# Half-filled score matmuls as pairs of 64-row tiles, in a one-core attention block on Trainium2

## The chip, the core and the metric

The kernel runs on one core of one Trainium2 chip. TensorE (PE) multiplies and writes its results to PSUM, eight banks of 512 f32 per partition. VectorE (DVE) and ScalarE (ACT) read PSUM and work on SBUF. POOL and SP mostly issue DMAs here. The metric is device time in microseconds, the median of the timed runs of a kernel. Whatever differs by less than 0.3% counts as no change that this measurement can tell.

## The reference

Eight batches of 112 query rows attend over a cache of 512 keys, with 32 heads of width 192. The projections before and after the attention belong to it.

```
B, Sq, D = 8, 112, 640;  H, Sk, Dh = 32, 512, 192          # all bf16
q      = (x @ wq).reshape(B, Sq, H, Dh).transpose(0, 2, 1, 3)
scores = einsum("bhqd,bhkd->bhqk", q, k_cache) * Dh ** -0.5
p      = softmax(scores, axis=-1)
o      = einsum("bhqk,bhkd->bhqd", p, v_cache)
out    = o.transpose(0, 2, 1, 3).reshape(B, Sq, H * Dh) @ wo
```

## The kernel before

The 32 heads are split into four groups of eight. Within a head group the kernel goes over the eight batches, and within a batch over four pairs of heads: 4 x 8 x 4 = 128 pairs, numbered `ip`. K and V come in groups of two pairs (four heads), 64 groups in all, each into one of six `kt` and six `vt` buffers.

All five engines run programs that are written out by hand in a fixed order. `DEFAULT_ORDERS` gives for each engine a list of stages with a lag, and in period i an engine runs each stage for pair i + lag. TensorE's list is S(i), PT0(i-1), PV(i-2), PT1(i-1), O(i-3), Q(i+2). VectorE's is smax0(i), smax1(i), qc(i+1), evacpT1(i-1), recip(i), diag0(i), diag1(i), oacc(i-3). ScalarE's is evacQ(i+1), evacpT0(i-1), exp0(i), exp1(i), evacPV(i-2). Semaphores hold the engines together: an instruction waits until a count of another engine's steps is reached, and whatever stands behind it on its engine waits with it. Nothing is reordered by a scheduler.

The stages of one pair (two heads h = 0, 1):

- **Q** (L262): 15 matmuls with 112 columns make the queries of both heads, 384 rows in three chunks, in PSUM bank 5. ScalarE copies them to slots 0 to 2 of the buffer `qs` (evacQ, L272).
- **qc** (L323 to L326): a head's 192 rows don't fill whole chunks of 128. The middle chunk, slot 1, holds the last 64 rows of head 0 in partitions 0 to 63 and the first 64 rows of head 1 in partitions 64 to 127. VectorE therefore moves half-chunks across partitions into slots 3 to 6 (L324, L325), and copies the halves of slot 1 into slots 7 and 8 (L323, L326). The other halves of slots 7, 8, 3 and 6 that a score matmul reads as padding are zeros: `qs` is set to zero at the start, and nothing is ever written there.
- **S** (L166 to L169): the scores. The transposing DMA leaves K in `kt[:, parity, m, :]` with keys of even and odd parity in the two halves of one 384-row stack: m = 0 holds 128 rows of the even keys, m = 2 holds 128 rows of the odd keys, and m = 1 holds the remaining 64 rows of the even keys in partitions 0 to 63 and of the odd keys in partitions 64 to 127. For each head there are four matmuls with 256 columns: even keys with m = 0 and m = 1 (L166, L167), odd keys with m = 2 and m = 1 (L168, L169). The two with m = 1 run over 128 partitions, but half of their stationary operand is zeros. Head h has bank h to itself.
- **smax0, smax1** (L332): VectorE reads bank h, scales it into `s_sb` and takes the row minimum. **exp** (ACT, L284) makes `p_sb` and the row sums. **recip** (L344) and **diag** (L308) make a diagonal matrix of the inverse sums.
- **PT** (L182): four matmuls per head transpose and scale the probabilities. ScalarE (L278) and VectorE (L338, evacpT1) copy them out.
- **PV** (L200, L206): eight matmuls with full 128-column tiles, then eight whose output has 64 partitions. The latter go in pairs to two column tiles of the array (h = 0 to partitions 0 to 63, h = 1 to 64 to 127). The profile writes their shape as 128\*64. ScalarE copies the result out (L291).
- **O** (L234, L235): six matmuls with `wo`, summed over four pairs; every fourth pair VectorE adds the sum to an accumulator (oacc, L375; L377 in the last head group).

S waits for the copies of its queries (`dQC`), for its K (`mK`) and for VectorE's reads of the banks of the pair before (`dSM`: the first head needs smax0 of the pair before, the second smax1). SP issues the K transposes (L477) and V loads (L489) alternately; a buffer's next load waits until its last use has passed. POOL issues the weights.

Of the kernel before, what the change touches and what calls it, by code (L numbers as in the profile page):

```python
# [9 lines left out]
ALU = mybir.AluOpType  # L10
# [10 lines left out]
def build_mha_kernel(nc, x, k_cache, v_cache, wq, wo, out, cfg=None):  # L21
    cfg = dict(cfg or {})
    B, SQ, D = x.shape
# [11 lines left out]
    G = 4  # L35
    NGRP = NPAIR // 2
    scale = float(DH) ** -0.5
# [14 lines left out]
    NSS = cfg.get("NSS", 4)  # L52
# [10 lines left out]

    EA = [0, 5]
    OC = [4, 2]
    ET = [7, 6]
    OH = [3, 8]
    NSLOT = 9

    with ExitStack() as es:  # L70
        def sb(name, shape, dt):
            return es.enter_context(nc.sbuf_tensor(name, shape, dt))

        def sem(name):
            return es.enter_context(nc.semaphore(name))
# [12 lines left out]
        kt = [sb(f"kt{j}", [128, 2, 3, G * 128], BF16) for j in range(NKB)]  # L88
        vt = [sb(f"vt{j}", [128, G, 768], BF16) for j in range(NVB)]
        qs = sb("qs", [128, NQ, NSLOT, SQ], BF16)  # L90
        s_sb = sb("s_sb", [SQ, NSS, SK], F32)
# [9 lines left out]
        ps = es.enter_context(nc.psum_tensor("ps", [128, 8, 512], F32))  # L101

        sS = sem("sS"); sPT = sem("sPT"); sPV = sem("sPV"); sO = sem("sO"); sQ = sem("sQ")
        dSM = sem("dSM"); dDG = sem("dDG"); dQC = sem("dQC"); dPTE = sem("dPTE"); dOA = sem("dOA"); dRC = sem("dRC")
# [41 lines left out]
        def W(eng, s, v):  # L146
            if v > 0:
                eng.wait_ge(s, v)
# [4 lines left out]
        def pe_S(pe, i):  # L153
            g = i // 2
            kb = g % NKB
            qb = i % NQ
            W(pe, dQC, i + 1)
            W(pe, mK[kb], 16 * (g // NKB + 1))
            for h in range(2):
                Hh = 2 * i + h  # L160
                u = Hh % G
                W(pe, dSM, Hh - 1)
                bk = ps[0:SQ, h, :]
                ktb = kt[kb]
                cs = slice(u * 128, (u + 1) * 128)
                pe.matmul(bk[:, 0:256], qs[:, qb, EA[h], :], ktb[:, :, 0, cs], start=True, stop=False)  # L166
                pe.matmul(bk[:, 0:256], qs[:, qb, ET[h], :], ktb[:, :, 1, cs], start=False, stop=True)  # L167
                pe.matmul(bk[:, 256:512], qs[:, qb, OC[h], :], ktb[:, :, 2, cs], start=True, stop=False)  # L168
                pe.matmul(bk[:, 256:512], qs[:, qb, OH[h], :], ktb[:, :, 1, cs], start=False, stop=True).then_inc(sS, 1)  # L169

        def pe_PT(pe, ip, h):
            Hh = 2 * ip + h
# [74 lines left out]
        def pe_Q(pe, ip):  # L247
# [11 lines left out]
            for c in range(3):  # L259
                for dc in range(DC):  # L260
# [3 lines left out]
            mm.then_inc(sQ, 1)  # L264

        PE_STAGES = dict(S=pe_S, PT0=lambda pe, ip: pe_PT(pe, ip, 0), PT1=lambda pe, ip: pe_PT(pe, ip, 1),
                         PV=pe_PV, O=pe_O, Q=pe_Q, OF=pe_OF)

# [44 lines left out]
        def dve_qc(eng, ip, as_i32=False):  # L313
            on_pool = as_i32
            if on_pool != (ip >= QC_SWITCH):
                return
            qb = ip % NQ
            if on_pool and ip == QC_SWITCH:
                W(eng, dQC, ip)
            W(eng, aQE, ip + 1)  # L320
            v = (lambda ap: ap.bitcast(mybir.dt.int32)) if as_i32 else (lambda ap: ap)
            f2 = lambda ap: v(ap.rearrange("p a b -> p (a b)"))
            eng.tensor_copy(v(qs[0:64, qb, 7, :]), v(qs[0:64, qb, 1, :]))  # L323
            eng.tensor_copy(f2(qs[0:64, qb, 4:7, :]), f2(qs[64:128, qb, 0:3, :]))  # L324
            eng.tensor_copy(f2(qs[64:128, qb, 3:6, :]), f2(qs[0:64, qb, 0:3, :]))  # L325
            eng.tensor_copy(v(qs[64:128, qb, 8, :]), v(qs[64:128, qb, 1, :])).then_inc(dQC, 1)  # L326

        def dve_smax(dve, i, h):
            Hh = 2 * i + h
            W(dve, sS, Hh + 1)  # L330
            W(dve, aEX, Hh - NSS + 1)
            dve.tensor_scalar(s_sb[:, Hh % NSS, :], ps[0:SQ, h, :], -scale, None, op0=ALU.mult,  # L332
                              op1=ALU.min, accum_out=nmx[:, Hh % NS:Hh % NS + 1]).then_inc(dSM, 1)

        def dve_evacpT1(dve, ip):
# [10 lines left out]
        def dve_oacc(dve, ip):  # L346
# [22 lines left out]
            for k, (src, cs) in enumerate(parts):  # L369
# [6 lines left out]
                else:  # L376
                    ins = dve.tensor_tensor(o_out[:, b, cs], src, acc[:, b, cs], op=ALU.add)  # L377
            ins.then_inc(dOA, 1)

        DVE_STAGES = dict(diag0=lambda d, ip: dve_diag(d, ip, 0), diag1=lambda d, ip: dve_diag(d, ip, 1),  # L380
                          qc=dve_qc, smax0=lambda d, i: dve_smax(d, i, 0), smax1=lambda d, i: dve_smax(d, i, 1),
                          evacpT1=dve_evacpT1, recip=dve_recip, oacc=dve_oacc)

# [153 lines left out]
        def _(gp):  # L537
# [107 lines left out]
            def pool_o(gp_, i):  # L645
                for fn in odmas.get(i, []):
                    fn()

            POOL_STAGES = dict(qc=lambda e, ip: dve_qc(e, ip, as_i32=True))
            pend = max(dmas) + 1  # L650
            wl = max([lag for st, lag in orders["POOL"] if st == "w"] + [0])
# [12 lines left out]
def bass_standalone__mha_block_cached__near_ridge_kernel(  # L664
    nc: bass.Bass,
    x: bass.AP,
    k_cache: bass.AP,
    v_cache: bass.AP,
    wq: bass.AP,
    wo: bass.AP,  # L670
    out: bass.AP,
):
    return build_mha_kernel(nc, x, k_cache, v_cache, wq, wo, out)
# [28 lines left out]
```

## Time and profile before

| what | value |
|---|---|
| timed runs | 500.34, 501.38, 502.07 us; median 501.38 |
| profiled execution: span from first to last instruction | 499.2 us, mean granted TensorE clock 0.999 |
| median of the timed runs less that span | 2.1 us |
| spacing of S(i) to S(i+1) on TensorE, median | 3.65 us |
| score matmuls L166, L167, L168, L169 | 256 each, recorded 275, 273, 272, 273 ns (medians) |
| qc copies L323, L324, L325, L326 in one period | 178, 243, 242, 189 ns |
| smax L332 | 685 ns, and an 82 ns read of the accumulator that overlaps the next instruction |

The profiler lists no total of the profiled execution apart from its span; the 2.1 us are what this document takes as lying around the span.

How to read it. In the timeline each row has its start in us from the span's start, its length in us, the engine, the line, the operation, what it writes and reads, the shape, and how many instructions the row merges; a note in square brackets tells of idle time ahead of it and of what ended that. TensorE's matmuls are pipelined, so a matmul recorded with 273 ns can start 109 ns after the one before; what a matmul costs is the distance between starts. Loads of the stationary operand are listed as an engine of their own (PEld).

### The profile page before, as it was taken

What the parts mean: (1) busy time and instruction counts of PE and PEld (TensorE: products, weight loads), DVE (VectorE), ACT (ScalarE), POOL (GpSimd) and SP (SyncE); (2) the same over time, 40 slices, a digit from 0 to 9 for tenths busy, and PEclk for the clock granted to TensorE, in tenths of its full rate; (3) what the DMA queues carried; (4) which work ended last, traced back from release to release, by engine and by line L of the source; (5) the groups of instructions that cost most, each with busy time, mean ns of one, the idle gap of its engine ahead of it and who ended that gap; (6) DMA issues with size and microseconds to landing.
All of it is one profiled execution on the core that took longest, in us unless ns stands there. A gap on an engine that the chain in (4) does not pass through costs nothing.

```text
span 499.2 us, 18678 instructions
## 1 busy us (share of the span) xinstructions
PE 479.0 (96%) x6824; PEld 418.9 (84%) x6824; DVE 446.6 (89%) x1610; ACT 355.1 (71%) x898; POOL 71.5 (14%) x133
## 2 busy tenths in 40 slices
PE   1799999999999999999999999999999999999995
PEld 1788888888888888888888888888888888888884
DVE  2589999998999999999999999999999999999994
ACT  1277777777777777777777777777777777777773
POOL 7110133131000133131000122322000000000000
PEclk9999999999999999999999999999999999999999
DMA  9999999999999999999999999999999999999000
GB/s 227 305 285 239 244 256 274 249 265 292 237 249 263 281 261 259 245 265 251 239 247 236 259 290 279 240 282 260 233 272 254 255 260 255 238 258 261 3 14 25
DMA packets 239738, 119.90 MB, mean 240 GB/s; under 512 B 201840, under 2 KB 236480, under 8 KB 239648
## 3 DMA queue, kind: packets, MB, share of 16 engines
q1 hardware_dynamic: 233472, 101.82, 94.4%
q0 software_dynamic: 6176, 16.88, 11.3%
q8 instruction: 56, 0.92, 0.8%
q14 instruction: 34, 0.28, 0.2%
HBM read 67.21 MB, written 1.15 MB: 137 GB/s over the span
## 4 chain that ended last, share of the span: by engine, by line
PE 93%; DMA 2%; issue 1%; DVE 1%; POOL 1%; ACT 0%; DVEq 0%; POOLq 0%; ACTq 0%
PE ps L262 19%; PE ps L234 16%; PE ps L182 13%; PE ps L200 10%; PE ps L206 8%; PE ps L166 6%; PE ps L169 6%; PE ps L167 6%; PE ps L168 6%; PE ps L235 4%; DMA wq_sb<-in_wq_dram 2%; DVE xT_sb L409 1%; POOL wq_sb L578 0%; DVE s_sb L332 0%; DVE o_out L377 0%
## 5 line engine op out<-in xcount | busy, mean ns | idle before, releaser
L284 ACT ACTIVATE p_sb<-s_sb,nmx 112x512 bf16<-112x512 f32 x256 | 181.6, 712 | 3.1 <-DVE s_sb L332 2.1
L332 DVE TENSOR_SCALAR_CACHE_REDUCE s_sb<-ps 112x512 f32<-112x512 f32 x256 | 166.3, 686 | 16.2 <-PE ps L169 14.0
L278 ACT ACTIVATE pT_sb<-ps 128x448 bf16<-128x448 f32 x128 | 69.5, 543 | 88.4 <-PE ps L182 88.4
L262 PE MATMUL ps<-xT_sb,wq_sb 128*128 128x112 bf16 x1920 | 118.0, 215 | 5.2 <-DMA wq_sb<-in_wq_dram 5.2
L234 PE MATMUL ps<-wo_sb,oT_sb 128*112 128x512 bf16 x384 | 118.3, 380 | 0.0
L262 PEld LDWEIGHTS ps<-xT_sb,wq_sb 128*128 128x128 bf16 x1920 | 103.8, 99 | 16.7 <-DMA wq_sb<-in_wq_dram 4.4
L182 PE MATMUL ps<-dg,p_sb 112*128 112x112 bf16 x1024 | 94.0, 214 | 1.8 <-ACT p_sb L284 1.6
L272 ACT ACTIVATE qs<-ps 128x336 bf16<-128x336 f32 x128 | 57.6, 450 | 45.0 <-PE ps L262 41.8
L338 DVE CAST pT_sb<-ps 128x448 bf16<-128x448 f32 x128 | 79.9, 624 | 5.3 <-PE ps L182 1.4
L235 PE MATMUL ps<-wo_sb,oT_sb 128*112 128x128 bf16 x384 | 83.9, 219 | 0.0
L182 PEld LDWEIGHTS ps<-dg,p_sb 112*128 112x128 bf16 x1024 | 64.5, 98 | 14.4 <-ACT p_sb L284 1.9
L166 PE MATMUL ps<-kt,qs 128*112 128x256 bf16 x256 | 70.8, 277 | 2.5 <-issue 1.9
L200 PE MATMUL ps<-pT_sb,vt 128*128 128x112 bf16 x1024 | 71.8, 213 | 0.1
L167 PE MATMUL ps<-kt,qs 128*112 128x256 bf16 x256 | 70.4, 275 | 0.0
L169 PE MATMUL ps<-kt,qs 128*112 128x256 bf16 x256 | 70.4, 275 | 0.0
L168 PE MATMUL ps<-kt,qs 128*112 128x256 bf16 x256 | 70.3, 275 | 0.0
L234 PEld LDWEIGHTS ps<-wo_sb,oT_sb 128*112 128x112 bf16 x384 | 49.7, 129 | 22.3
L581 POOL DMA_DIRECT2D wq_sb<-in_wq_dram x60 | 32.1, 539 | 188.5 <-DMA kt<-in_k_cache_dram 182.4
L308 DVE TENSOR_SCALAR dg<-ident,rinv 112x112 bf16<-112x112 bf16 x256 | 52.9, 249 | 5.0 <-issue 0.5
L200 PEld LDWEIGHTS ps<-pT_sb,vt 128*128 128x128 bf16 x1024 | 56.5, 98 | 0.9 <-issue 0.5
L291 ACT ACTIVATE oT_sb<-ps 128x336 bf16<-128x336 f32 x128 | 55.3, 432 | 1.7 <-PE ps L206 1.7
L235 PEld LDWEIGHTS ps<-wo_sb,oT_sb 128*112 128x112 bf16 x384 | 50.0, 130 | 0.0
(38 smaller groups left out, 498.5 us busy)
## 6 DMA issues: line engine op xcount, KB each, us to landing
vt<-in_v_cache_dram SPq DMA_DIRECT2D x64, 768.0 KB, 5.8
wq_sb<-in_wq_dram POOLq DMA_DIRECT2D x60, 96.0 KB, 5.3
wo_sb<-in_wo_dram POOLq DMA_DIRECT2D x24, 160.0 KB, 5.6
wo_sb<-in_wo_dram POOLq DMA_DIRECT2D x32, 80.0 KB, 5.1
wq_sb<-in_wq_dram POOLq DMA_DIRECT2D x4, 480.0 KB, 10.2
wo_sb<-in_wo_dram POOLq DMA_DIRECT2D x4, 320.0 KB, 10.9
out_dram<-o_out SPq DMA_DIRECT2D x8, 140.0 KB, 4.4
kt<-in_k_cache_dram SPq DMA_TRANSPOSE x64, 9.9
```

Of the source, the lines that this page charges most:

```text
L166: pe.matmul(bk[:, 0:256], qs[:, qb, EA[h], :], ktb[:, :, 0, cs], start=True, stop=False)
L167: pe.matmul(bk[:, 0:256], qs[:, qb, ET[h], :], ktb[:, :, 1, cs], start=False, stop=True)
L168: pe.matmul(bk[:, 256:512], qs[:, qb, OC[h], :], ktb[:, :, 2, cs], start=True, stop=False)
L169: pe.matmul(bk[:, 256:512], qs[:, qb, OH[h], :], ktb[:, :, 1, cs], start=False, stop=True).then_inc(sS, 1)
L182: mm = pe.matmul(ps[:, 2 + h, j * SQ:(j + 1) * SQ], p_sb[:, pslot, j * 128:(j + 1) * 128], dg[:, dslot, :], start=True, stop=True)
L200: pe.matmul(ps[:, 4, oc * SQ:(oc + 1) * SQ], vtb[:, u, q * 192: q * 192 + 128], pT_sb[:, ptb, h, j * SQ:(j + 1) * SQ], start=(j == 0), sto ...
L234: pe.matmul(ps[0:SQ, 6, :], oT_sb[:, ob, c, :], wo_sb[:, wb, 3 * lp + c, 0:512], start=first, stop=last)
L235: mm = pe.matmul(ps[0:SQ, 7, 0:128], oT_sb[:, ob, c, :], wo_sb[:, wb, 3 * lp + c, 512:640], start=first, stop=last)
L262: mm = pe.matmul(ps[:, 5, c * SQ:(c + 1) * SQ], lhsT, xT_sb[:, dc, b * SQ:(b + 1) * SQ], start=(dc == 0), stop=(dc == DC - 1))
L284: act.activation(p_sb[:, Hh % NP, :], s_sb[:, Hh % NSS, :], ACTF.Exp, bias=nmx[:, Hh % NS:Hh % NS + 1], scale=-1.0, accum_out=rsum[:, Hh % ...
L332: dve.tensor_scalar(s_sb[:, Hh % NSS, :], ps[0:SQ, h, :], -scale, None, op0=ALU.mult, op1=ALU.min, accum_out=nmx[:, Hh % NS:Hh % NS + 1]). ...
L338: dve.tensor_copy(pT_sb[:, ip % NPT, 1, :], ps[:, 3, 0:4 * SQ]).then_inc(dPTE, 1)
```

## The change

The two halves of chunk m = 1 are no longer padded to 128 rows. The four matmuls with m = 1 become 64-row matmuls: for the even keys on partitions 0 to 63, for the odd keys on partitions 64 to 127. The even keys of both heads go to bank 0, the odd keys of both to bank 1 (head h in columns 256h to 256h + 255), so that the two 64-row tiles of a pair write to different banks. The order within S becomes: four full matmuls (even and odd keys of head 0, then of head 1), then the four 64-row ones (even, odd, even, odd). Only the first matmul of a bank carries the start flag.

Both banks are complete only after the last matmul of S. So smax0 and smax1 both wait for all of S, each reads 256 columns of both banks, and S waits ahead of its first matmul for both smax of the pair before. The copies to slots 7 and 8 go, and `qs` has seven slots.

```diff
-    ET = [7, 6]
-    OH = [3, 8]
-    NSLOT = 9
+    ET = [1, 6]
+    OH = [3, 1]
+    NSLOT = 7
...
+            ktb = kt[kb]
+            cs = [slice(u * 128, (u + 1) * 128) for u in ((2 * i) % G, (2 * i + 1) % G)]
+            W(pe, dSM, 2 * i)
             for h in range(2):
-                Hh = 2 * i + h
-                u = Hh % G
-                W(pe, dSM, Hh - 1)
-                bk = ps[0:SQ, h, :]
-                ktb = kt[kb]
-                cs = slice(u * 128, (u + 1) * 128)
-                pe.matmul(bk[:, 0:256], qs[:, qb, EA[h], :], ktb[:, :, 0, cs], start=True, stop=False)
-                pe.matmul(bk[:, 0:256], qs[:, qb, ET[h], :], ktb[:, :, 1, cs], start=False, stop=True)
-                pe.matmul(bk[:, 256:512], qs[:, qb, OC[h], :], ktb[:, :, 2, cs], start=True, stop=False)
-                pe.matmul(bk[:, 256:512], qs[:, qb, OH[h], :], ktb[:, :, 1, cs], start=False, stop=True).then_inc(sS, 1)
+                hs = slice(h * 256, (h + 1) * 256)
+                pe.matmul(ps[0:SQ, 0, hs], qs[:, qb, EA[h], :], ktb[:, :, 0, cs[h]], start=(h == 0), stop=False,
+                          skip_group_check=True)
+                pe.matmul(ps[0:SQ, 1, hs], qs[:, qb, OC[h], :], ktb[:, :, 2, cs[h]], start=(h == 0), stop=False,
+                          skip_group_check=True)
+            for h in range(2):
+                hs = slice(h * 256, (h + 1) * 256)
+                m1 = pe.matmul(ps[0:SQ, 0, hs], qs[0:64, qb, ET[h], :], ktb[0:64, :, 1, cs[h]],
+                               start=False, stop=True, skip_group_check=True)
+                m2 = pe.matmul(ps[0:SQ, 1, hs], qs[64:128, qb, OH[h], :], ktb[64:128, :, 1, cs[h]],
+                               start=False, stop=True, skip_group_check=True)
+            m1.then_inc(sS, 1)
+            m2.then_inc(sS, 1)
...
-            eng.tensor_copy(v(qs[0:64, qb, 7, :]), v(qs[0:64, qb, 1, :]))
             eng.tensor_copy(f2(qs[0:64, qb, 4:7, :]), f2(qs[64:128, qb, 0:3, :]))
-            eng.tensor_copy(f2(qs[64:128, qb, 3:6, :]), f2(qs[0:64, qb, 0:3, :]))
-            eng.tensor_copy(v(qs[64:128, qb, 8, :]), v(qs[64:128, qb, 1, :])).then_inc(dQC, 1)
+            eng.tensor_copy(f2(qs[64:128, qb, 3:6, :]), f2(qs[0:64, qb, 0:3, :])).then_inc(dQC, 1)
...
-            W(dve, sS, Hh + 1)
+            W(dve, sS, 2 * i + 2)
...
-            dve.tensor_scalar(s_sb[:, Hh % NSS, :], ps[0:SQ, h, :], -scale, None, op0=ALU.mult,
+            dve.tensor_scalar(s_sb[:, Hh % NSS, :].rearrange("p (e c) -> p e c", e=2), ps[0:SQ, 0:2, h * 256:(h + 1) * 256], -scale, None, op0=ALU.mult,
```

## The prediction

> **What bounds the kernel now.** I read the page's busy shares first, then the chain that ended last, then one period of TensorE and of VectorE in the timeline, then the landings of K.
>
> ```profile
> PE 479.0 (96%) x6824; PEld 418.9 (84%) x6824; DVE 446.6 (89%) x1610; ACT 355.1 (71%) x898; POOL 71.5 (14%) x133
> ...
> PE 93%; DMA 2%; issue 1%; DVE 1%; POOL 1%; ACT 0%; DVEq 0%; POOLq 0%; ACTq 0%
> ```
>
> TensorE carries 93% of the chain. VectorE's 89% comes close, so it has to be asked whether it becomes the bound. The timeline of TensorE, one period:
>
> ```profile
> 241.87 0.28 PE L166 MATMUL ps<-kt,qs 128*112 128x256 bf16 x1
> 241.98 0.27 PE L167 MATMUL ps<-kt,qs 128*112 128x256 bf16 x1
> ...
> 242.75 0.36 PE L182 MATMUL ps<-dg,p_sb 112*128 112x112 bf16 x4
> 242.94 0.56 PE L200 MATMUL ps<-pT_sb,vt 128*128 128x112 bf16 x8
> 243.44 0.39 PE L206 MATMUL ps<-pT_sb,vt 128*64 128x112 bf16 x8
> 243.75 0.37 PE L182 MATMUL ps<-dg,p_sb 112*128 112x112 bf16 x4
> 243.96 0.38 PE L234 MATMUL ps<-wo_sb,oT_sb 128*112 128x512 bf16 x1
> ...
> 245.52 0.28 PE L166 MATMUL ps<-kt,qs 128*112 128x256 bf16 x1
> ```
>
> The reader is to see the distances between starts. The eight score matmuls take 242.75 - 241.87 = 0.88 us, 0.11 each (from single starts: 0.109), with no gap. A 112-column matmul costs 0.049 (the four of L182 from 242.75 to 242.94). The period is 3.65 us.
>
> The same rows hold the one place where this kernel already changes its tiles: L206 runs in pairs on two column tiles. Eight L200 at 0.049 would end at 243.33; L206 starts at 243.44, so going in costs **0.10**. L206 then needs 0.31 for four pairs; four starts at 0.049 are 0.20, and 0.11 more passes. In single starts: last L200 to first L206 0.143 instead of 0.049 (+0.094); first pair to second 0.074 instead of 0.049 (+0.025, the first load of 64 columns with nothing to hide behind); last pair to L182 0.145 instead of 0.049 (+0.096); L182's first step 0.060 (+0.011). The two matmuls of a pair start 0.003 to 0.004 apart: they do run side by side.
>
> K is the second limit, early on. The PE row, and below it the landing of the K load that SP issued at 81.17 for this group:
>
> ```profile
> 93.99 0.29 PE L166 MATMUL ps<-kt,qs 128*112 128x256 bf16 x1 [0.31 <-issue]
> ```
> ```profile
> DMA to landing us min/median/max: 12.7/12.7/12.7
> ```
>
> 81.17 + 12.7 = 93.9: K lands 0.1 before its use, and TensorE stood idle for it. The same holds for each group from 10 to 14 (uses at 93.99, 101.49, 109.22, 117.03, 124.68; excess over the usual spacing 0.48, 0.20, 0.42, 0.51, 0.34, together 1.95 us). Up to pair 28, at 124.7 us, the DMA queue sets the pace, whatever TensorE needs. After that K runs ahead: group 45, issued at 331.22 and landed at 344.06, is used at 351.44, and the last lands 26 us ahead.
>
> **The change, part by part**, per pair of heads.
>
> Removed on TensorE: four half-filled matmuls become two pairs. If a pair takes one slot of 0.109, as L206's pairs take one, two slots go: **-0.218**.
>
> Added on TensorE: two changes of tile shape, ahead of the first 64-row matmul and behind the last. No run of a 64-row tile is in this trace. The nearest rows are the ones above: +0.094 going in, +0.096 coming out, +0.011 at L182's first load, and the first load in the new shape. That load has 112 columns where L206 has 64, so I scale: 0.025 x 112 / 64 = 0.044. Sum **+0.245**. Bounds: nothing below, if rows can be split without waiting; above, if each change waits until the last matmul is recorded as ended (0.273 - 0.109 = 0.164 instead of 0.095 each), +0.14, and if the two loads of a pair go one after the other, +0.044. I take the values of L206: same array, same period, and its two changes agree within 0.002.
>
> Net: -0.218 + 0.245 = **+0.027 us a pair**. The array work that is saved is spent on the changes. L206 itself shows such a balance: with its changes it takes from 242.94 + 8 x 0.049 = 243.33 to 243.75, 0.42, where eight unpaired slots would take 0.39.
>
> The Trainium skill has rules on both sides. "TensorEngine Tiling (Array Packing)", Key Properties, says that a change of tiling mode, unlike a change of tile, drains the engine; the row of L206 agrees and gives it a price, 0.094 and 0.096. The same page's Theoretical Speedup gives up to 2x for 64 contraction rows; by that rule alone the sum would be -0.218 x 99 = -21.6 us, by the drain as priced here +2.7.
>
> Removed on VectorE: the copies L323 and L326, by starts 0.191 and 0.218, together **0.41 us** a period.
>
> ```profile
> 243.89 0.18 DVE L323 COPY qs<-qs 64x112 bf16<-64x112 bf16 x1
> 244.08 0.24 DVE L324 COPY qs<-qs 64x336 bf16<-64x336 bf16 x1
> ...
> 244.59 0.19 DVE L326 COPY qs<-qs 64x112 bf16<-64x112 bf16 x1
> 244.81 0.62 DVE L338 CAST pT_sb<-ps 128x448 bf16<-128x448 f32 x1
> ```
>
> None of it is on the path: VectorE's order needs 3.32 us a pair and 0.8 for oacc every fourth, 3.5 on average against 3.65. It only widens this slack.
>
> Added on VectorE: smax0 starts after all of S. It began at 242.67; all of S is done at 242.64 + 0.27 = 242.91 at the earliest, some 0.3 later. Behind it wait smax1, qc, evacpT1, recip and both diags, and ScalarE's exps; the two missing copies give 0.41 back from evacpT1 on. Does TensorE feel it? From the end of S: 0.3 + 0.61 + 0.61 + two copies 0.51 makes `dQC` at about 2.0 us; the next S starts 2.77 after the end of this one. evacpT1 0.66, recip 0.20, diag0 0.25: diag0 at 3.1, needed by PT0 at 3.65. The first head's S must now wait for smax1, done at 1.6. All have over 0.5 us to spare, so **nothing**. smax itself reads the same 512 elements in two runs; a third more for each (0.23 + 0.23) would still fit. With that cover gone it would cost its excess over 0.5 a period.
>
> The smaller clearing of `qs` (1.3 us at the start) lies beside the first weights' DMA: nothing.
>
> **The sum.** To pair 28 K sets the pace: 28 x 0.027 = 0.8 us more work goes into the 1.95 us of idle time. From there 99 pairs x 0.027 = +2.7 us. Span 499.2 + 2.7 = 501.9, and with 2.1 around it 504.0; the same sum on the median, 501.4 + 2.7 = 504.1. I say **504.1 us**.
>
> **The rivals.**
>
> *No wait between shapes (the fast one).* Only the pairs count: -0.218 a pair, capped by K. Group 45 landed at 344.06 and so can be used at most 7.3 us earlier than now; TensorE alone would be 62 x 0.218 = 13.5 ahead by then. 7.3 + the last 37 x 0.218 = 8.1 makes -15.4: **486**. For it: a row split leaves the output columns of the array as they are, and the rows of before show only the column kind. Against it: S would be the second user of tiles, and the first one pays at both ends. It decides as soon as both changes and the load cost under 0.218 together.
>
> *Half a price.* Only one change waits, or a 64-row tile drains sooner: -0.02 to -0.12 a pair, 99 of them: **489 to 499**. If a tenth less than 0.245 is paid, it comes out even: 500 to 503.
>
> *Heavier changes.* Loads of a pair one after the other (+0.044), or waits up to the recorded ends (+0.14): +0.06 to +0.17 a pair; over 99 pairs +6 to +17, and on the first 28 little, since idle time takes it up to 0.07 a pair: **507 to 519**.
>
> *The pairs don't overlap* (the change doesn't do what it says). Then the 0.218 is not saved: +0.245 x 99 = 24.3, and 28 x 0.245 - 1.95 = 4.9 ahead of them: **531**. Against it: the pairs of L206 start 0.003 apart.
>
> **How the numbers follow.** Forecast (503 to 507): 0.47. Heavier (507 to 519): 0.15, most of it below 514. No overlap: 0.06. Even: 0.09. Half a price: 0.13. No wait: 0.10. Leaving out no wait, no overlap and the top of the heavier case (0.03) leaves the range **489 to 514**. With 0.3% (1.5 us) as what a measurement can tell: faster 0.23, within 0.09, slower 0.68.
>
> **What would show it.** In the timeline after: the four full matmuls 0.109 apart; the last of them to the first 64-row matmul about 0.20; the two of a pair 0.004 apart; first pair to second 0.15; last pair to PT0 0.20; S 0.90 instead of 0.88, the period 3.67. VectorE: smax0 waits for S in nearly every period (14.0 us in 42 waits now), with its busy time down by about 50 us. I am wrong if the steps between shapes are near 0.109, if the two of a pair start 0.1 apart, or if TensorE waits for VectorE ahead of S or PT0.

## The result and the profile after

The changed kernel takes 502.59 us against 500.35 for the one before, both medians of 18 runs: a ratio of **1.0036, with a 95% interval of 1.0020 to 1.0052**. The ratio is that of the means, 502.35 against 500.54: it is slower, by 1.8 us of 500 (the medians differ by 2.2). That is just above the 0.3% that this measurement can tell, and the interval reaches below it. The forecast was 504.1 on 501.4, or 1.0054. The direction was right; the added time was 1.5 times too large, and the reason for that is worth more than the size. Of the 1.5 us between 504.1 and 502.59, 1.0 is no part of the forecast change: the prediction started from 501.38, the median of three runs, and 18 runs give 500.35.

The page of the kernel after, busy shares and the chain that ended last:

```profile
PE 477.9 (95%) x6824; PEld 375.2 (75%) x6824; DVE 399.3 (80%) x1354; ACT 357.2 (71%) x898; POOL 71.5 (14%) x133
...
PE 92%; DMA 5%; issue 1%; DVE 1%; POOL 0%; ACT 0%; DVEq 0%; POOLq 0%; ACTq 0%
```

VectorE lost 47 us of work (446.6 to 399.3) and TensorE still carries the chain. One period of TensorE after (columns as in the prediction):

```profile
242.37 0.28 PE L164 MATMUL ps<-kt,qs 128*112 128x256 bf16 x1
242.48 0.27 PE L166 MATMUL ps<-kt,qs 128*112 128x256 bf16 x1
242.59 0.27 PE L164 MATMUL ps<-kt,qs 128*112 128x256 bf16 x1
242.70 0.27 PE L166 MATMUL ps<-kt,qs 128*112 128x256 bf16 x1
242.90 0.31 PE L170 MATMUL ps<-kt,qs 64*112 64x256 bf16 x1
242.90 0.31 PE L172 MATMUL ps<-kt,qs 64*112 64x256 bf16 x1
243.05 0.27 PE L170 MATMUL ps<-kt,qs 64*112 64x256 bf16 x1
243.06 0.27 PE L172 MATMUL ps<-kt,qs 64*112 64x256 bf16 x1
243.26 0.37 PE L188 MATMUL ps<-dg,p_sb 112*128 112x112 bf16 x4
...
246.04 0.28 PE L164 MATMUL ps<-kt,qs 128*112 128x256 bf16 x1
```

The pairs do run side by side: 242.90 and 242.90, 243.05 and 243.06. And both changes of shape can be seen: 0.20 from 242.70 to 242.90, where full matmuls are 0.11 apart, and 0.20 from 243.06 to 243.26. S takes 0.89 us instead of 0.88, the period 3.67 instead of 3.65.

VectorE after:

```profile
242.38 0.41 DVE L314 TENSOR_SCALAR dg<-ident,rinv 112x112 bf16<-112x112 bf16 x2
243.39 0.69 DVE L336 TENSOR_SCALAR_CACHE_REDUCE s_sb<-ps 112x512 f32<-112x512 f32 x1 [0.61 <-PE ps L172]
...
244.74 0.24 DVE L329 COPY qs<-qs 64x336 bf16<-64x336 bf16 x1
244.99 0.24 DVE L330 COPY qs<-qs 64x336 bf16<-64x336 bf16 x1
245.27 0.62 DVE L342 CAST pT_sb<-ps 128x448 bf16<-128x448 f32 x1
```

It now waits 0.61 us for the end of S, as the changed waits demand, and has two copies instead of four. smax in its new form takes 0.69, as before.

To see where the time went, take the starts of S in each trace and cut the run at pairs 4, 28 and 126 (the last full period):

| kernel | median spacing | pairs 4 to 28 | pairs 28 to 126 | spacings over median + 0.03, pairs 28 to 126 |
|---|---|---|---|---|
| before | 3.647 us | 89.7 us | 358.5 us | 7 |
| after | 3.669 us | 88.9 us | 359.6 us | 0 |

After pair 28 the median grew by 98 x 0.022 = 2.2 us, but the stretch by only 1.1. Of before's 358.5 us, 98 x 3.647 = 357.4 is the regular spacing and 1.1 is **irregular periods that are not there after the change**. Six of the seven are the periods of pairs 56, 68, 84, 92, 100 and 116, every one a multiple of four; together they hold 0.8 us. The seventh, at pair 47, is a single stall of 0.29. The prediction had put nothing there.

### The profile page after: what moved, and what is told of

Read it like the earlier page. It is cut to its first block, busy times and chain, and to the rows that moved or that the text cites. A ratio compares the mean times of both kernels' runs of the same rounds, so it can differ in the third digit from the quotient of the medians.

```text
span 500.6 us, 18422 instructions
## 1 busy us (share of the span) xinstructions
PE 477.9 (95%) x6824; PEld 375.2 (75%) x6824; DVE 399.3 (80%) x1354; ACT 357.2 (71%) x898; POOL 71.5 (14%) x133
## 3 DMA queue, kind: packets, MB, share of 16 engines
q0 software_dynamic: 6176, 16.88, 10.7%
## 4 chain that ended last, share of the span: by engine, by line
PE 92%; DMA 5%; issue 1%; DVE 1%; POOL 0%; ACT 0%; DVEq 0%; POOLq 0%; ACTq 0%
PE ps L268 18%; PE ps L240 16%; PE ps L188 15%; PE ps L206 10%; PE ps L170 9%; PE ps L212 8%; PE ps L164 6%; PE ps L166 5%; PE ps L241 4%; DMA kt<-in_k_cache_dram 3%; DMA wq_sb<-in_wq_dram 2%; DVE s_sb L336 0%; DVE o_out L381 0%; ACT p_sb L290 0%; POOL wq_sb L582 0%
## 5 line engine op out<-in xcount | busy, mean ns | idle before, releaser
L188 PE MATMUL ps<-dg,p_sb 112*128 112x112 bf16 x1024 | 95.1, 216 | 1.7 <-ACT p_sb L290 1.6
L188 PEld LDWEIGHTS ps<-dg,p_sb 112*128 112x128 bf16 x1024 | 54.6, 98 | 34.7 <-issue 22.8
L206 PE MATMUL ps<-pT_sb,vt 128*128 128x112 bf16 x1024 | 72.1, 213 | 0.7 <-issue 0.7
L164 PE MATMUL ps<-kt,qs 128*112 128x256 bf16 x256 | 64.0, 277 | 5.1 <-DMA kt<-in_k_cache_dram 4.2
L166 PE MATMUL ps<-kt,qs 128*112 128x256 bf16 x256 | 63.5, 275 | 0.0
L206 PEld LDWEIGHTS ps<-pT_sb,vt 128*128 128x128 bf16 x1024 | 57.2, 98 | 1.1 <-issue 1.1
L172 PE MATMUL ps<-kt,qs 64*112 64x256 bf16 x256 | 54.6, 294 | 0.0
L170 PE MATMUL ps<-kt,qs 64*112 64x256 bf16 x256 | 54.6, 294 | 0.0
```

The lines of the kernel that those rows point to most:

```text
L164: pe.matmul(ps[0:SQ, 0, hs], qs[:, qb, EA[h], :], ktb[:, :, 0, cs[h]], start=(h == 0), stop=False, skip_group_check=True)
L166: pe.matmul(ps[0:SQ, 1, hs], qs[:, qb, OC[h], :], ktb[:, :, 2, cs[h]], start=(h == 0), stop=False, skip_group_check=True)
L170: m1 = pe.matmul(ps[0:SQ, 0, hs], qs[0:64, qb, ET[h], :], ktb[0:64, :, 1, cs[h]], start=False, stop=True, skip_group_check=True)
L188: mm = pe.matmul(ps[:, 2 + h, j * SQ:(j + 1) * SQ], p_sb[:, pslot, j * 128:(j + 1) * 128], dg[:, dslot, :], start=True, stop=True)
L206: pe.matmul(ps[:, 4, oc * SQ:(oc + 1) * SQ], vtb[:, u, q * 192: q * 192 + 128], pT_sb[:, ptb, h, j * SQ:(j + 1) * SQ], start=(j == 0), sto ...
```

## The experiments

The theory after the result: the changes of tile shape cost what they seem to, and the two copies were *not* beside the path, because VectorE came late around every fourth pair. The rival: the copies cost nothing, and the missing part of the 2.7 us was taken up by the start and by K's pace. Ratios are to the kernel before on the same chip, with 95% intervals.

### The copies alone

The tiles stay as before; the padded matmuls that read slots 7 and 8 now read slot 1 whole. One matmul of each head (L167 of the first, L169 of the second; not two, as the text below has it) then also takes in 64 rows of the other head, so the scores are not those of the reference: this kernel leaves out needed work and serves for its time alone.

```diff
-    ET = [7, 6]
-    OH = [3, 8]
-    NSLOT = 9
+    ET = [1, 6]
+    OH = [3, 1]
+    NSLOT = 7
...
-            eng.tensor_copy(v(qs[0:64, qb, 7, :]), v(qs[0:64, qb, 1, :]))
             eng.tensor_copy(f2(qs[0:64, qb, 4:7, :]), f2(qs[64:128, qb, 0:3, :]))
-            eng.tensor_copy(f2(qs[64:128, qb, 3:6, :]), f2(qs[0:64, qb, 0:3, :]))
-            eng.tensor_copy(v(qs[64:128, qb, 8, :]), v(qs[64:128, qb, 1, :])).then_inc(dQC, 1)
+            eng.tensor_copy(f2(qs[64:128, qb, 3:6, :]), f2(qs[0:64, qb, 0:3, :])).then_inc(dQC, 1)
```

> The kernel before without the copies to slots 7 and 8: the score matmuls keep all 128 rows and read slot 1 whole, so two of the four products per head also take in 64 rows of the other head. Theory (VectorE was on the path): the median spacing of S stays 3.647 us, but the longer periods after pair 28 vanish; pair 28 to 126 takes 98 x 3.647 = 357.4 us instead of 358.5, and the ratio to before is 0.997 to 0.999. Rival (the copies are beside the path, and what was missing of the +2.7 us was taken up by the start and K's pace): longer periods remain, ratio 1.000 within 0.001.

Measured: **0.9955 (0.9937 to 0.9974)**, 2.2 us less. Median spacing 3.645; pairs 28 to 126 take 357.2 us, with no spacing over the median by 0.03. The theory holds and the rival falls. The gain is larger than the 0.1% to 0.3% that I gave it, though its interval reaches down to 0.26%. The profiles place 1.1 to 1.3 us of it in the pairs from 28 on; where the rest lies is not shown.

### The copies back on VectorE

The kernel after, with both copies made again.

```diff
-    NSLOT = 7
+    NSLOT = 9
...
+            eng.tensor_copy(v(qs[0:64, qb, 7, :]), v(qs[0:64, qb, 1, :]))
             eng.tensor_copy(f2(qs[0:64, qb, 4:7, :]), f2(qs[64:128, qb, 0:3, :]))
-            eng.tensor_copy(f2(qs[64:128, qb, 3:6, :]), f2(qs[0:64, qb, 0:3, :])).then_inc(dQC, 1)
+            eng.tensor_copy(f2(qs[64:128, qb, 3:6, :]), f2(qs[0:64, qb, 0:3, :]))
+            eng.tensor_copy(v(qs[64:128, qb, 8, :]), v(qs[64:128, qb, 1, :])).then_inc(dQC, 1)
```

> The kernel after with the two copies put back (nothing reads them). Theory: VectorE needs 3.5 us a pair again and starts each pair 0.3 us later than in before, so TensorE waits for it around every fourth pair (the accumulation of O): one period in four of 3.75 to 4.0 us, the others 3.67; ratio to before 1.008 to 1.03. Rival: periods of 3.67 as in after, ratio 1.003 to 1.005.

Measured: **1.0223 (1.0199 to 1.0246)**, 1.9% above after. Spacing 3.67 in three periods of four and mostly 3.97 in the fourth. Who waited, in the view of waits (times: total, number, longest):

```profile
PE ps L188 <- issue: 5.9, 31, 0.3
...
ACT p_sb L290 <- DVE s_sb L338: 13.4, 31, 1.8
```

31 waits in 128 pairs: one in four, the periods after the accumulation of O. The profile does not name the releaser of TensorE's wait ("issue"). The two timelines do, VectorE's diagonals and TensorE's PT0:

```profile
261.71 0.41 DVE L314 TENSOR_SCALAR dg<-ident,rinv 112x112 bf16<-112x112 bf16 x2
```
```profile
262.06 0.36 PE L188 MATMUL ps<-dg,p_sb 112*128 112x112 bf16 x4 [0.19 <-issue]
```

The first diagonal takes 0.25 and ends at 261.96; PT0 starts 0.10 later. That 0.10 is the handover: in every fourth pair of this run it is 0.102 or 0.103. So 0.41 us of VectorE's time per pair was the cover that the change itself needed: without it, 31 x 0.30 = 9.3 us, which is what was measured (511.88 against 502.59, and 1.9% by the ratios).

### The copies on ScalarE

The kernel before, with slots 7 and 8 written from PSUM by ScalarE.

```diff
             act.activation(qs[:, ip % NQ, 0:3, :], ps[:, 5, 0:3 * SQ].rearrange("p (c s) -> p c s", c=3),
-                           ACTF.Copy).then_inc(aQE, 1)
+                           ACTF.Copy)
+            act.activation(qs[0:64, ip % NQ, 7, :], ps[0:64, 5, SQ:2 * SQ], ACTF.Copy)
+            act.activation(qs[64:128, ip % NQ, 8, :], ps[64:128, 5, SQ:2 * SQ], ACTF.Copy).then_inc(aQE, 1)
...
-            eng.tensor_copy(v(qs[0:64, qb, 7, :]), v(qs[0:64, qb, 1, :]))
             eng.tensor_copy(f2(qs[0:64, qb, 4:7, :]), f2(qs[64:128, qb, 0:3, :]))
-            eng.tensor_copy(f2(qs[64:128, qb, 3:6, :]), f2(qs[0:64, qb, 0:3, :]))
-            eng.tensor_copy(v(qs[64:128, qb, 8, :]), v(qs[64:128, qb, 1, :])).then_inc(dQC, 1)
+            eng.tensor_copy(f2(qs[64:128, qb, 3:6, :]), f2(qs[0:64, qb, 0:3, :])).then_inc(dQC, 1)
```

> The kernel before with the two copies to slots 7 and 8 made by ScalarE from PSUM instead of by VectorE. Theory (what the change gained lies in freeing VectorE, nothing of it in the tiles): spacing 3.645 without longer periods, ratio to before 0.994 to 0.998, as with the copies left out. Rival (ScalarE, at 2.8 us a pair and then some 3.2, comes late with the exps): longer periods stay, ratio 1.000 or above.

Measured: **0.9953 (0.9935 to 0.9970)**, the same as without the copies. Pairs 28 to 126 take 357.4 us, none longer. The gain that hid in the change needs no tiles at all, and ScalarE has room for the work.

### Four changes of shape instead of two

```diff
                 pe.matmul(ps[0:SQ, 1, hs], qs[:, qb, OC[h], :], ktb[:, :, 2, cs[h]], start=(h == 0), stop=False,
                           skip_group_check=True)
-            for h in range(2):
-                hs = slice(h * 256, (h + 1) * 256)
                 m1 = pe.matmul(ps[0:SQ, 0, hs], qs[0:64, qb, ET[h], :], ktb[0:64, :, 1, cs[h]],
```

> The kernel after with each head's two 64-row matmuls right after its two full ones, so that the tile shape changes four times within S instead of twice. Theory (a change costs what after shows: 0.093 in, 0.092 out, and 0.041 for each first load of 112 columns): +0.267 us a pair, spacing 3.94 us, ratio to before 1.07. Rival (part of the cost is paid once per S, or hides): spacing 3.75 to 3.85.

Measured: **1.0692 (1.0656 to 1.0727)**, spacing 3.943: +0.274 a pair. TensorE in this run:

```profile
243.27 0.27 PE L166 MATMUL ps<-kt,qs 128*112 128x256 bf16 x1
243.48 0.31 PE L168 MATMUL ps<-kt,qs 64*112 64x256 bf16 x1
243.48 0.31 PE L170 MATMUL ps<-kt,qs 64*112 64x256 bf16 x1
243.72 0.32 PE L164 MATMUL ps<-kt,qs 128*112 128x256 bf16 x1
243.88 0.27 PE L166 MATMUL ps<-kt,qs 128*112 128x256 bf16 x1
...
244.33 0.37 PE L186 MATMUL ps<-dg,p_sb 112*128 112x112 bf16 x4
```

Each pair of tiles pays on its own: 0.20 going in, 0.24 from the pair to the next full matmul, and 0.15 (the median; 0.16 here) from that one to the one behind it, where it is 0.11 in after. The first matmuls after a change take 0.15 until the next start in both kernels, in after from the first pair to the second. So the 0.24 can be read as these 0.15 and 0.09 for the change back. Nothing is paid once per S; the price is per change.

### One tile twice, then the other

The order even, even, odd, odd, to see whether tiles overlap only with their neighbours in the program.

```diff
                 m1 = pe.matmul(ps[0:SQ, 0, hs], qs[0:64, qb, ET[h], :], ktb[0:64, :, 1, cs[h]],
                                start=False, stop=True, skip_group_check=True)
+            for h in range(2):
+                hs = slice(h * 256, (h + 1) * 256)
                 m2 = pe.matmul(ps[0:SQ, 1, hs], qs[64:128, qb, OH[h], :], ktb[64:128, :, 1, cs[h]],
```

> The kernel after with the 64-row matmuls in the order even, even, odd, odd (one tile twice, then the other twice). Theory (a tile's own matmuls queue, different tiles overlap, all in order): three slots of 0.109 instead of two, spacing 3.669 + 0.109 = 3.78 us. Rivals: 3.67 if the order doesn't matter, 3.89 if only a fresh pair overlaps.

Measured, in one run: spacing 3.673, as in after. The theory missed by 0.11 a pair; of these two orders neither is the slower. TensorE:

```profile
244.57 0.27 PE L166 MATMUL ps<-kt,qs 128*112 128x256 bf16 x1
244.78 0.31 PE L170 MATMUL ps<-kt,qs 64*112 64x256 bf16 x1
244.78 0.31 PE L174 MATMUL ps<-kt,qs 64*112 64x256 bf16 x1
244.93 0.27 PE L170 MATMUL ps<-kt,qs 64*112 64x256 bf16 x1
244.94 0.27 PE L174 MATMUL ps<-kt,qs 64*112 64x256 bf16 x1
```

L170 is issued twice before L174, but the first L174 starts with the first L170 (single starts: 0.006 later), ahead of the second.

### Two kinds of tiles side by side

If a change costs 0.09 whatever the shapes, S's row tiles should be followed by PV's column tiles: three changes a pair instead of four. PT0 moves behind PV, the column tiles to PV's head, and on VectorE the accumulation of O goes ahead of the reciprocals (the later PT0 makes room for it there).

```diff
-    PE=[("S", 0), ("PT0", -1), ("PV", -2), ("PT1", -1), ("O", -3), ("Q", 2)],
+    PE=[("S", 0), ("PV", -2), ("PT0", -1), ("PT1", -1), ("O", -3), ("Q", 2)],
...
-    DVE=[("smax0", 0), ("smax1", 0), ("qc", 1), ("evacpT1", -1), ("recip", 0), ("diag0", 0), ("diag1", 0),
-         ("oacc", -3)],
+    DVE=[("smax0", 0), ("smax1", 0), ("qc", 1), ("evacpT1", -1), ("oacc", -3), ("recip", 0),
+         ("diag0", 0), ("diag1", 0)],
...
```

> The kernel after with TensorE's stages in the order S, PV, PT0, PT1, O, Q, and within PV the column tiles first, so that S's 64-row tiles are followed directly by PV's column tiles; on VectorE the accumulation of O goes ahead of the reciprocals. Theory (a change of shape costs about 0.09 whatever the two shapes are): three changes a pair instead of four, spacing 3.58 us, no waits for VectorE, ratio to before 0.978 to 0.984. Rival 1 (from row tiles to column tiles costs twice, as if by way of the full shape): 3.68, ratio 1.000 to 1.006. Rival 2 (the later PT0 makes TensorE wait for VectorE or ScalarE): spacing over 3.7 in some periods, ratio over 0.99.

Measured: **0.9822 (0.9791 to 0.9852)**, 492.6 us, the fastest version here: 1.8% below before and some 2.1% below after. Spacing 3.562. TensorE:

```profile
244.06 0.27 PE L172 MATMUL ps<-kt,qs 64*112 64x256 bf16 x1
244.26 0.39 PE L205 MATMUL ps<-pT_sb,vt 128*64 128x112 bf16 x8
244.58 0.57 PE L212 MATMUL ps<-pT_sb,vt 128*128 128x112 bf16 x8
244.99 0.56 PE L188 MATMUL ps<-dg,p_sb 112*128 112x112 bf16 x8
```

From row tiles to column tiles it takes 0.20 (single starts 0.199, less the 0.109 of the matmul itself: 0.090), no more than from row tiles to full ones. One change and the loads behind it are saved: 3.669 - 3.562 = 0.107. Over 126 pairs that would be 13.5 us below after; about 10.7 were measured. The profile, taken of the fastest of the six runs (489.67), shows where some of it goes: K lands only 0.09 us ahead of its use at groups 12 to 14, which costs 1.0 us, and three longer periods hold 0.65 more.

The same with VectorE's old order:

> As the run with the tiles together, but with VectorE's order of before, the accumulation of O last. Theory: with three changes of shape the typical spacing is 3.58 too, but every fourth period S waits for VectorE, which comes to smax and the copies 0.8 us late: 3.8 to 4.0 us there; ratio 0.99 to 1.005. Rival (VectorE is off the path now that two copies are gone): every period 3.58, ratio as in the other run.

Measured: 0.9890 (0.9859 to 0.9922), 0.7% more than with the accumulation moved. The periods go 3.56, 3.56, 3.64, 3.60: VectorE is late once in four again, by less than I expected (0.1 instead of 0.2 to 0.4): in these periods S's first load starts 0.05 us after VectorE's last copy of the queries ends, in the others 0.65. How much slack VectorE has depends on where in its order the accumulation stands.

### Second profiles of both kernels

> The kernel before, unchanged, for a second profile. If K's landing sets the pace up to pair 28 as the prediction said, S again waits for K at pairs 20 to 28, and pairs 4 to 28 take some 89.7 us. If that was a chance of one run's start, they take 24 x 3.647 = 87.5 us plus what VectorE costs, and K lands over 1 us ahead. From pair 28 to 126, under the theory of VectorE, again over 358 us with longer periods at every fourth pair.

> The kernel after, unchanged, for a second profile. Theory: spacing 3.669, pairs 28 to 126 in 98 x 3.669 = 359.6 us with no longer period. If K's landing sets the pace up to pair 28 whatever TensorE needs, S waits for K there; if not, pairs 4 to 28 take 88.1 us.

| kernel | median spacing | pairs 4 to 28 | pairs 28 to 126 | spacings over median + 0.03, pairs 28 to 126 |
|---|---|---|---|---|
| before, again | 3.647 us | 87.6 us | 358.4 us | 8 |
| after, again | 3.669 us | 88.1 us | 360.4 us | 1 |

Before's irregular periods are there again, at much the same pairs (the one at pair 100 is 3.90 in both profiles), while after has one, of 4.49, with a single stall of 0.82 between two matmuls of O. But K's pace is not: in this run of before, K landed 1.7 to 3.6 us ahead of its use at groups 10 to 14, and S never waited for it after pair 3. In the second profile of after the lead was 0.7 to 1.7 us, also without a wait. So K's waits up to pair 28, on which the prediction built, come in some runs and not in others. Of all the profiles here only two more show them, those of the two versions with the tiles together, whose shorter periods also need K sooner. What decides it in before is not shown.

## Why the prediction was wrong in size

**The net of the tiles: right, a little high.** The prediction said -0.218 + 0.245 = +0.027 us a pair; the median spacing grew by 0.022. In single starts after: last full matmul to first tile 0.202 (forecast 0.203), first pair to second 0.153 (0.153), last pair to PT0 0.201 (0.205), offset of a pair 0.003 to 0.004. The rows of L206, scaled from 64 to 112 columns, gave all of it within 0.004. L182's first step had been 0.053 before, not 0.049, so that of the 0.011 only 0.007 was new. Over 126 pairs 0.022 is 2.8 us.

The Trainium skill's rule that a change of tiling mode drains the engine ("TensorEngine Tiling (Array Packing)", Key Properties) agrees with what is measured here for row tiles, in that each change adds a wait, of 0.093 and 0.092.

**"None of it is on the path": the step that failed.** The prediction weighed VectorE's average, 3.5 us a pair against 3.65, concluded that taking 0.41 off it "only widens this slack", and put the term at nothing. The copies alone, taken away, bring 2.2 us (1.3 to 3.1). The average hides that the 0.8 us of oacc falls on one pair in four: behind it everything on VectorE is late, and diag0, which TensorE's PT0 needs, comes in at the last moment. It could have been read in before, in the very period that the prediction showed and in VectorE's rows ahead of it:

```profile
238.55 0.88 DVE L375 TENSOR_TENSOR acc<-ps,acc 112x512 f32<-112x512 f32 x2
239.35 0.68 DVE L332 TENSOR_SCALAR_CACHE_REDUCE s_sb<-ps 112x512 f32<-112x512 f32 x1
...
242.34 0.41 DVE L308 TENSOR_SCALAR dg<-ident,rinv 112x112 bf16<-112x112 bf16 x2
```
```profile
242.67 0.28 PEld L182 LDWEIGHTS ps<-dg,p_sb 112*128 112x128 bf16 x4
```

The first of the two diagonals takes 0.25 and ends at 242.59; PT0 (L182) started at 242.75. With a handover of 0.10 that leaves 0.05 us of slack. PT0's load of its operand has none: in 23 of the 24 such pairs from 28 to 126 it starts 0.07 us after diag0's end, against 0.37 to 0.52 (medians) in the other pairs, so in nearly every fourth pair this load already stood waiting for VectorE. Over before's later pairs the time from diag0's end to PT0's matmul runs 0.62, 0.15, 0.47, 0.62, again and again; after it is 0.63 or more in all but a few pairs, with the copies left out 0.75 or more, again in all but a few. The prediction's estimate, diag0 at 3.1 us after the end of S against 3.65 for PT0, took VectorE as starting smax0 on time, which after oacc it didn't: smax0 starts 0.64 us after S in two pairs of four, 1.12 in the pair behind oacc (at 239.35 above, where S started at 238.22) and still 0.80 in the next one. With the copies left out it is 0.93 and then 0.64 again.

What the late load then does to the matmuls is shown only in part. Of the 0.8 us in before's six irregular fourth periods, some 0.3 stand ahead of PT0, and 0.5 ahead of the first matmul of PV, which is next in TensorE's order. At pair 100 the load for PT0 starts 0.07 after diag0's end, yet its matmul 0.30 later; why is not shown, and the version with the tiles together has a stall of 0.31 behind S of the same pair, although what PV needs there had been ready for 0.46. So this one may not be VectorE's. What is shown is that these periods go when VectorE is early: in both versions of before without the copies on VectorE, and in after, they are absent.

**The 28 pairs that K was to hide: wrong too, the other way.** They were to take up 0.8 us. The second profiles show that K doesn't set the pace there in general, so these pairs pay as well: in them, pairs 4 to 28 take 88.1 us against 87.6.

The sum with measured terms: +2.8 for the tiles, -2.2 (between -3.1 and -1.3) for the copies, makes +0.6, between -0.3 and +1.5; measured +1.8, between 1.0 and 2.6. The two overlap; the middles differ by 1.2 us, and the runs don't settle whether that is more than the noise. After against the copies left out (1.0036 against 0.9955) is 4.0 us, and the two intervals allow 2.3 to 5.8, where 126 x 0.024 gives 3.0. By the profiles alone it fits: 126 x 0.022 = 2.8 for the tiles, less the 0.8 to 1.1 of before's irregular periods, is +1.7 to +2.0.

**The rivals.** No wait between shapes, half a price, and pairs without overlap are refuted by the rows of after; heavier changes too. The measured 502.59 lies in the band of the prediction's even case, 500 to 503, but not by that case's reason, a tenth less than 0.245 for the changes: the rows give 0.24, and what brings the time down is the lower baseline and VectorE's term. On the cover that smax0's later start needs, the prediction was right: with the copies gone, TensorE doesn't wait for it although smax0 starts later. With them back it does, for 9.3 us.

## What to carry to other kernels

Halving the array work of a few matmuls pays only if what is saved is more than two changes of tile shape: here 0.218 us of 256-column slots against 0.24. Count the changes in a period, and put the tiled groups side by side: that turned +0.4% into -1.1%, and into -1.8% with the accumulation moved on VectorE as well. And where an engine's load is uneven over the periods, don't judge its slack by the mean: look at the period behind the heavy one, and measure from its last instruction to the one that waits for it.

## What the hardware showed that was not expected

- The price of a change of tile shape hardly depended on which shapes: 0.093 from full to row tiles, 0.092 back, 0.090 from row to column tiles, 0.093 to 0.096 between full and column tiles, each on top of the matmul's own time. The first matmuls after a change took 0.04 us longer until the next start, with loads of 112 columns.
- Matmuls on different row tiles need not be neighbours in the program to overlap: issued as even, even, odd, odd they started as even, odd, even, odd, the first odd one 0.006 us after the first even one. This was seen in one run.
- Single stalls of 0.3 to 0.9 us between two matmuls of one stage, where the program has no wait, turned up in some profiles (0.29 at 195.58 us in before, 0.89 at 52.9 us in after). Their cause was not looked for.
